# Gated product and attention sum kept in PSUM, chunk-0 scores by heads at partitions 0 and 64, and a new order list, in an mLSTM-then-gated-FFN kernel

## Chip, cores and metric

One core of a Trainium2 chip. The metric is device time in microseconds; the kernel before takes 550.04 us (median of 3 runs).

## The reference

Two stages. The first is an mLSTM over 768 steps for 4 batches and 8 heads of width 40, the second a gated feed-forward layer on its output (3072 tokens, 320 features, 1536 hidden).

```
for t in range(S):
    m_new = maximum(f[t] + m, i[t]);  fs = exp(f[t] + m - m_new);  is_ = exp(i[t] - m_new);  m = m_new
    C = fs * C + is_ * v_t k_t^T;     n = fs * n + is_ * k_t
    y[t] = sigmoid(o[t]) * (C q_t) / max(|n . q_t|, 1)
x    = y rearranged to (B*S, H*D)
out  = (sigmoid(x @ w_gate) * (x @ w_val)) @ w_out
```

## The kernel before

Time is cut into 6 chunks of 128 steps (c). A *unit* n = 4c + b is one chunk of one batch b: 24 units, each with all 8 heads. Within a chunk the recurrence is turned into attention: scores of k against q, times a decay matrix `d`, times v (with a column of ones for the denominator), plus, from chunk 1 on, the part that comes from the carried state `cst`. The output of a unit, 128 tokens, is split into two fp32r parts `xh` and `xl`, which the feed-forward layer multiplies with weights that are split in the same way.

Each operation is a small function with a name, and the list `ORDER` names all of them in the order in which they are recorded. Each engine runs its own instructions in that order, waiting for what they read and for the buffers that they write. The names that matter here (n a unit or a tile, g a group of heads, x a half):

- `lq`, `lk`, `lv`, `lo`, `ld`: loads of q, k, v, the output gate and the decay's row maxima, on SP's queue (the first q on ACT's). `wd..`, `wa..`, `wb..`, `wc..`, `wo..`, `wh..`, `wl..`: load and split of a piece of the weights (letter g, v, r, o: gate, value, the last 64 features of both, output).
- `tr n.g`: TensorE transposes of q and k of a group of heads to PSUM (`pt`); `cp n.g`: copy to SBUF (`qkt`); `qb n.g`: the q of the group, repeated per head and multiplied by a mask, so that it becomes block-diagonal (`qbd`); `s n.g`: the scores, one fp32 matmul per group of 3, 3 and 2 heads (`GROUPS`). Chunks 0 and 1 work like this. From chunk 2 on (`tq`, `tw`, `sr`, `sh`, `sl`) q and k are transposed by way of DRAM, and `sl` (L662) finishes an exact split on DVE.
- `sp`, `ee`, `em`: decay of units 0 and 1; `t n.g`: scores times decay, on DVE (L777); `dl`, `kw`: k times the last decay column, for the state; `cs`, `cm`, `cd`, `ca`: state update; `in`, `ti`: state part of the output, in tile `t`; `av n`: decay-weighted scores times v (L837, L844).
- `ad n` (L852): `t` + `av`; `nd n`: the denominator, three small DVE steps; `ns n`: times the output gate; `ro n`: divided; `xd`, `xt`, `xh`, `xl`: transpose and split of the result.
- feed-forward tile n (128 hidden features j, and 2 or 4 units, so 256 or 512 tokens): `u0`, `r0`: 8 matmuls for the gate into bank `pg0`; `u1`, `r1`: 8 for the value into `pg1`; `th`: tanh of the gate to tile `sg` (L977, ACT); `gx`: (sg + 1) * value (L981, DVE); `gh`: its high part (L986, ACT); `gl`: the rest (L991, DVE); `dn n.t`: three matmuls per unit into the output bank `po t`. `ob`: output to DRAM.

PSUM has eight banks: `po0` to `po3`, `pg0`, `pg1`, and `pa0`, `pa1`, which take turns for everything else. Some early operations borrow the first six (`POPEN`). `sg` has one buffer, `gh` and `gl` two. `wm` is 8 matmuls on zeros, whose result nobody reads. In chunk 0 the masks of unit 0 (three) and one each of units 1, 2 and 3 run on DVE, the other six on POOL.

Of the kernel before, what the change touches and what calls it, by code (L numbers as in the profile page):

```python
# [8 lines left out]
F32 = mybir.dt.float32  # L9
# [18 lines left out]
    'BC': 2,  # L28
    'warm': 8,
# [14 lines left out]
    qb1.2 wdo3 cp2.0 lq4 dl1 wbg0 xd0 s1.1 l11 wdv1 wcg0 wog0 whv0 wlo1 whg0 tr2.1 og1 t1.0 ld3 cp2.1 s1.2 t1.2 t1.1
    wlv0 xt0 xh0 xl0 wdv2 ee2.1 qb2.1 av1 wao3 wbo3 ns1 qb2.0 s2.0 nd1 em2 ro1 wlg0 xd1 dl2 xt1 wav1 wco3 wao2 ee3.0
    t2.0 xh1 kw1 wbv1 tr2.2 cp2.2 lq6 woo3 who3 l12 kw2 wlo3 wag1 xl1 u1.0 ee3.1 lo4 cs1 cm1.0 wbo2 wco2 wcv1 cm1.1
    woo2 wov1 lv4 l14 whv1 wbg1 u0.0 em3 tr3.0 r0.0 wcg1 ld4 who2 cp3.0 tr3.1 wlo2 qb2.2 wog1 wdo4 r1.0 cp3.1 th0
    tr3.2 s2.2 gx0 cp3.2 lo2 t2.2 gh0 s2.1 t2.1 lk4 dl3 tbp tbc wlv1 og2 qb3.1 wao4 ee4.0 whg1 wbo4 wlg1 u0.1 av2
    tr4.1 lv3 l13 wco4 lo3 gl0 qb3.2 og4 og3 woo4 r0.1 u1.1 ns2 th1 who4 qb3.0 nd2 tr4.0 cp4.0 cp4.1 r1.1 wdr1 wlo4
    ld6 war1 s3.1 t3.1 wav2 s3.0 wbr1 t3.0 ee4.1 wdv3 qb4.0 tr4.2 gx1 qb4.1 u0.2 s3.2 t3.2 ro2 cp4.2 av3 ee6.1 gd  # L50
    cs2 wcr1 u1.2 xd2 ns3 nd3 lk5 wbv2 tdp wcv2 dn0.0 gh1 cm2.0 cm2.1 wor1 wov2 tdc em4 dl4 wdo5 s4.1 qb4.2 t4.1
    wdr2 lv5 s4.0 t4.0 dn0.1 s4.2 whr1 wdg4 xt2 t4.2 wao5 xh2 xl2 wbo5 wlr1 r1.2 lq5 wco5 woo5 r0.2 kw4 cs4 whv2
    war2 av4 l15 cm4.0 wdr3 cm4.1 gl1 in4 kw3 wbr2 wcr2 who5 ro3 xd3 i6 wlv2 th2 u0.3 wdg3 wor2 wlo5 dn1.0 dn1.1 ti4
    wdo7 gx2 u1.3 r0.3 gh2 ad4 xt3 gl2 ld5 r1.3 tr5.0 dn2.0 th3 xh3 dn2.1 gx3 xl3 u0.4 wav3 wag4 cp5.0 r0.4 tr5.1
    gh3 whr2 wbv3 wcv3 wov3 wdg2 cs3 gl3 wbg4 u1.4 r1.4 cp5.1 whv3 dn3.0 th4 gx4 u0.5 r0.5 dn3.1 gh4 gl4 th5 tep
    u1.5 r1.5 dn4.2 wcg4 wlr2 wao7 wog4 gx5 u0.6 wbo7 dn4.3 r0.6 wlv3 wag2 u1.6 wbg2 wcg2 r1.6 ee5.0 gh5 wog2 whg2
    gl5 dn5.3 dn5.2 th6 u0.7 r0.7 wco7 gs4 gx6 u1.7 wlg2 r1.7 gh6 gl6 ns4 th7 gs5 woo7 nd4 whg4 gx7 lq8 wlg4 u0.8
    cm3.0 cm3.1 gh7 gl7 wdv5 dn6.2 who7 u1.8 r0.8 qb5.0 wag3 wbg3 wlo7 qb5.1 dn6.3 dn7.3 th8 r1.8 war3 wbr3 u0.9
    dn7.2 r0.9 gx8 wcr3 wcg3 wog3 wdv4 ro4 wor3 wdo6 gh8 gl8 s5.1 u1.9 r1.9 whg3 wlg3 whr3 wlr3 th9 dn8.1 wav4 lk6
    gs2 tec gx9 wbv4 dn8.2 gh9 lo5 cd4.0 dn8.3 wdo8 u0.10 wcv4 cd4.1 ca4.1 dn8.0 ee6.0 ee5.1 tr5.2 r0.10 wov4 u1.10  # L60
    r1.10 whv4 gl9 wao6 dn9.3 wbo6 lo6 th10 lv6 wao8 em5 wco6 dl5 gx10 woo6 u0.11 dn9.0 r0.11 wdr4 u1.11 dn9.1 r1.11
    kw5 dn9.2 who6 wlv4 wbo8 wco8 wdg5 woo8 gh10 gl10 who8 wlo8 war4 wlo6 th11 wav5 t5.1 xd4 gx11 wbr4 wcr4 s5.0
    cp5.2 u0.12 wbv5 dn10.0 wor4 t5.0 wdo9 qb5.2 whr4 wlr4 dn10.2 lk7 dn10.3 gh11 em6 in5 tr6.0 ti5 cp6.0 wcv5 wov5
# [127 lines left out]
def mlstm_then_gated_ffn_kernel(  # L191
# [87 lines left out]
    taken["gh"] = 1  # L279

    @op("wz")
    def _():
        nc.vector.memset(warm, 0.0)
# [248 lines left out]
    def unit(n):  # L532
# [313 lines left out]
        def hs():  # L846
            return t1s[n] if c > 0 else pv_[n]
# [207 lines left out]
```

## Time and profile before

| | |
|---|---|
| runs | 550.04 us median of 3 (548.8 to 552.62) |
| profiled execution, as timed / its span | 546.66 us / 544.9 us |
| TensorE (PE) | 518.4 us busy, 95% |
| VectorE (DVE) | 360.5 us, 66% |
| ScalarE (ACT) | 248.0 us, 46% |
| GpSimdE (POOL) | 266.2 us, 49% |
| moved by DMA | 74.15 MB, mean 136 GB/s |
| granted clock, mean | 0.984 |

Busy is the time in which an engine has an instruction in work. A row of the order of time reads: start, duration, engine, line, operation, output <- inputs, shape, count, and in brackets how long the engine stood idle just before and what ended that. A row of a group has, behind the bar, busy time, mean of one in ns, idle time before them and its releasers. A row of waits has the time in all, the times and the longest.

### The profile page before, as it was taken

The page shows a single profiled execution, that of the slowest core. Times are in us where ns is not written, and L with a number is a line of the kernel's source. Part 1 is how long each engine was busy: PE and PEld are TensorE (multiplying, and loading weights), DVE is VectorE, ACT ScalarE, POOL GpSimd, SP SyncE. Part 2 cuts the span into 40 slices and gives each one's busy share as a digit, 9 for nine tenths or more (in the row PEclk, how much of TensorE's full clock was granted, in tenths as well). Part 3 has the DMA queues.
Part 4 walks back from the last instruction along what each step waited for, and adds up shares of the span by engine and source line. Part 5 has one row for each costly group of instructions (what it writes and reads, how often), then busy time and mean ns, then how long its engine had stood idle before and what let it go on. Part 6 is the DMA issues. An engine that isn't in the chain of part 4 may idle for free.

```text
span 544.9 us, 10878 instructions
## 1 busy us (share of the span) xinstructions
PE 518.4 (95%) x3957; PEld 472.7 (87%) x3957; DVE 360.5 (66%) x702; ACT 248.0 (46%) x564; POOL 266.2 (49%) x299
## 2 busy tenths in 40 slices
PE   5889999999989999989989999999999979999997
PEld 4668998889989999988778888888888878899997
DVE  7888877777877667657767467677555675744232
ACT  4867666654525453553432444441444322423222
POOL 2767555748464564574763756835502436421000
PEclk9959999999999999999998999999999999999999
DMA  9985836467587878696684779775786485221000
GB/s 209 254 226 138 235 86 147 125 143 171 159 156 147 166 169 173 119 201 148 145 173 92 161 164 188 143 128 128 133 162 118 85 153 103 52 38 50 6 14 36
DMA packets 222477, 74.15 MB, mean 136 GB/s; under 512 B 167380, under 2 KB 214168, under 8 KB 222424
## 3 DMA queue, kind: packets, MB, share of 16 engines
q1 hardware_dynamic: 221336, 73.20, 62.4%
q8 instruction: 31, 0.51, 0.4%
q10 hardware_dynamic: 1088, 0.26, 0.3%
q14 instruction: 22, 0.18, 0.1%
HBM read 61.54 MB, written 11.90 MB: 135 GB/s over the span
## 4 chain that ended last, share of the span: by engine, by line
PE 69%; DMA 13%; SPq 6%; DVE 5%; issue 3%; ACT 3%; POOL 1%; ACTq 0%; DVEq 0%; POOLq 0%
PE pg L967 28%; PE po L1001 6%; PE po L1003 6%; PE po L1002 6%; PE pg L971 5%; PE pg L972 5%; DMA scx<-tx 3%; DMA qs<-scq 3%; PE av L837 2%; PE s L679 2%; DMA d<-mscr 2%; PE s L713 2%; PE av L844 2%; PE in L820 2%; SPq L650 1%
## 5 line engine op out<-in xcount | busy, mean ns | idle before, releaser
L967 PE MATMUL pg<-xh,wh 128*128 128x256 f32 (+1 forms) x412 | 106.8, 341 | 6.7 <-ACT sg L977 5.6
L981 DVE SCALAR_TENSOR_TENSOR sg<-sg,pg 128x256 f32<-128x256 f32 (+1 forms) x103 | 53.8, 523 | 74.7 <-PE pg L972 50.0
L986 ACT ACTIVATE gh<-sg 128x256 fp32r<-128x256 f32 (+1 forms) x103 | 51.7, 502 | 112.3 <-DVE sg L981 83.8
L967 PE MATMUL pg<-xh,wl 128*128 128x256 f32 (+1 forms) x412 | 101.8, 329 | 0.0
L967 PE MATMUL pg<-xl,wh 128*128 128x256 f32 (+1 forms) x412 | 101.7, 328 | 0.0
L977 ACT ACTIVATE sg<-pg 128x256 f32<-128x256 f32 (+1 forms) x103 | 48.1, 467 | 109.5 <-PE pg L972 54.5
L991 DVE TENSOR_TENSOR gl<-sg,gh 128x256 fp32r<-128x256 f32 (+1 forms) x103 | 71.1, 690 | 40.1 <-ACT gh L986 39.8
L1001 PE MATMUL po<-oh,gh 128*128 128x320 f32 x288 | 92.3, 321 | 0.0
L1003 PE MATMUL po<-oh,gl 128*128 128x320 f32 x288 | 89.5, 311 | 0.5 <-DVE gl L991 0.5
L1002 PE MATMUL po<-ol,gh 128*128 128x320 f32 x288 | 89.1, 309 | 0.0
L967 PEld LDWEIGHTS pg<-xh,wh 128*128 128x128 f32 x412 | 67.9, 191 | 12.8 <-ACT sg L977 7.7
L967 PEld LDWEIGHTS pg<-xl,wh 128*128 128x128 f32 x412 | 69.8, 191 | 7.5 <-POOL xl L910 0.6
L967 PEld LDWEIGHTS pg<-xh,wl 128*128 128x128 f32 x412 | 69.9, 191 | 7.1
L971 PE MATMUL pg<-xh,w 128*128 128x256 f32 (+1 forms) x206 | 69.2, 338 | 0.0
L972 PE MATMUL pg<-xl,w 128*128 128x256 f32 (+1 forms) x206 | 67.0, 327 | 0.0
L1001 PEld LDWEIGHTS po<-oh,gh 128*128 128x128 f32 x288 | 54.5, 189 | 2.7
L1002 PEld LDWEIGHTS po<-ol,gh 128*128 128x128 f32 x288 | 54.3, 189 | 2.8
L1003 PEld LDWEIGHTS po<-oh,gl 128*128 128x128 f32 x288 | 54.2, 188 | 1.0 <-DVE gl L991 1.0
L793 POOL TENSOR_TENSOR dr<-d 128x1024 f32<-128x1024 f32 x16 | 31.8, 1986 | 44.5 <-DVE d L777 44.5
L777 DVE TENSOR_TENSOR d<-s,d 128x384 f32<-128x384 f32 (+1 forms) x72 | 35.5, 504 | 12.6 <-PE s L679 7.0
L612 POOL TENSOR_TENSOR d<-at,d 128x1024 f32<-128x1024 f32 x16 | 33.0, 2068 | 21.8 <-DMA d<-mscr 17.4
L620 POOL TENSOR_SCALAR_AFFINE_SELECT d<-d 128x1024 f32<-128x1024 f32 x22 | 25.9, 1180 | 36.0 <-ACT d L616 31.9
(151 smaller groups left out, 936.1 us busy)
## 6 DMA issues: line engine op xcount, KB each, us to landing
d<-mscr SPq DMA_DIRECT2D x22, 512.0 KB
ks<-scq SPq DMA_DIRECT2D x48, 168.0 KB
qs<-scq SPq DMA_DIRECT2D x48, 168.0 KB
scq<-tq SPq DMA_DIRECT2D x64, 80.0 KB
k<-in_k_dram SPq DMA_DIRECT2D x24, 160.0 KB
su_o<-in_moe_w_out_dram SPq DMA_DIRECT2D x12, 320.0 KB
v<-in_v_dram SPq DMA_DIRECT2D x24, 160.0 KB
o<-in_o_gate_dram SPq DMA_DIRECT2D x24, 160.0 KB
```

Source lines behind the costliest of these rows:

```text
L612: E("ea", n).tensor_tensor(dm[n], a, dm[n], ALU.subtract)
L777: nc.vector.tensor_tensor(y, ps_[n, g][:, :nh, :], y, ALU.mult)
L967: nc.tensor.matmul(p, w[y][:, a, fs], x[c][:, a, n0:n1], start=(i + a == 0), stop=False)
L971: nc.tensor.matmul(pg[n, y], w2[y][:, fs], xh[c][:, 2, n0:n1], start=False, stop=False)
L972: nc.tensor.matmul(pg[n, y], w2[y][:, fs], xl[c][:, 2, n0:n1], start=False, stop=True)
L977: nc.scalar.activation(s, pg[n, 0], AF.Tanh, scale=0.5)
L981: nc.vector.scalar_tensor_tensor(sgs[n], sgs[n], 1.0, pg[n, 1], ALU.add, ALU.mult)
L986: nc.scalar.activation(ghs[n][:, :nt], sgs[n], AF.Copy)
L991: E("gl", n).tensor_tensor(gls[n][:, :nt], sgs[n], ghs[n][:, :nt].bitcast(F32), ALU.subtract)
L1001: nc.tensor.matmul(p, ghs[n][:, ts], oh[:, j, :], start=(j == 0), stop=False)
L1002: nc.tensor.matmul(p, ghs[n][:, ts], ol[:, j, :], start=False, stop=False)
L1003: nc.tensor.matmul(p, gls[n][:, ts], oh[:, j, :], start=False, stop=(j == NF - 1))
```

## The change

Four parts.

1. `gx` writes its product over the value in `pg1`; `gh` and `gl` read it from there. `sg` is then read only by `gx`.
2. `ad` writes its sum over `av` in PSUM; `nd` and `ns` read it there.
3. In chunk 0, q and k are loaded with each head's 40 columns padded to 64 (the pads are zeroed by DVE, `pz`; the tiles borrow buffers of `xh`, `xl`, `gl`, `gh` and `sg`). A transpose takes two heads, which come to lie at partitions 0 and 64; there are four for q and four for k of a unit, into two banks. A score matmul takes one head from partitions 0 to 39 or 64 to 103 and writes to one of two banks. `qb`, the third group of `tr`, `cp`, `s` and `t`, and the block-diagonal q go for these units. `kw` writes to a new tile.
4. A new `ORDER`, and other borrowed banks. The parameters `CA` and the per-half lookup for `cd` are there and change nothing.

```diff
+    'GX': 1, 'AD': 1, 'CA': 0, 'PAD': 1,
...
+        pads = []
+        for x, tags in enumerate((("xh1",), ("xl1",), ("gl0", "gl1"), ("gh1", "sg0"))):
+            ts = [sb.tile([P, 2 // len(tags), H, DP], F32, tag=t, name=f"pad{x}{y}") for y, t in enumerate(tags)]
+            pads.append([ts[y][:, 0] if len(tags) == 2 else ts[0][:, y] for y in range(2)])
+        @op("pz")
+            for w in pads[0] + pads[1] + pads[2] + pads[3]:
+                nc.vector.memset(w[:, :, D:], 0.0)
...
     POPEN = {
         "sp0.0": "po0", "sp0.1": "po1", "sp1.0": "po2", "sp1.1": "po3",
-        "tr0.2": "pg0", "tr1.0": "pg0", "tr1.1": "pg1", "s0.0": "pg1", "s1.0": "po1", "s1.1": "po2", "s1.2": "po3",
-        "av0": "po0", "av1": "pg0",
+        "s0.0": "pg0", "s0.1": "pg1", "s1.0": "po0", "s1.1": "po1", "av0": "pg0", "av1": "pg1",
...
+            for x in range(2):                                      # tr, cp of a padded unit
+                    pt_[n, x] = p = pst(P_(f"tr{n}.{x}"), [P, 4, L], f"pt_{n}_{x}")
+                    for y in range(4):
+                        nc.tensor.transpose(p[:, y, :], pads[n][x][:, 2 * y : 2 * y + 2, :].rearrange("p h d -> p (h d)"), ident)
...
+            @op(f"s{n}.0")
+                for x in range(2):
+                    ps_[n, x] = pst(P_(f"s{n}.{x}"), [P, 4, L], f"s_{n}_{x}")
+                for y in range(4):
+                    for x in range(2):
+                        rs = slice(DP * x, DP * x + D)
+                        nc.tensor.matmul(ps_[n, x][:, y, :], sop[n][rs, 1, y, :], sop[n][rs, 0, y, :], start=True, stop=True)
...
-                y = dm[n][:, h0 : h0 + nh, :]
+                y = dm[n][:, g::2, :] if padded else dm[n][:, h0 : h0 + nh, :]
                 nc.vector.tensor_tensor(y, ps_[n, g][:, :nh, :], y, ALU.mult)
...
+                if padded:
+                    kt[n] = sbt("k", [P, H, D], F32, f"k_{n}", 3)
...
-            return t1s[n] if c > 0 else pv_[n]
+            return t1s[n] if c > 0 and not PARAM["AD"] else pv_[n]
...
-                nc.vector.tensor_tensor(t1s[n], t1s[n], pv_[n], ALU.add)
+                nc.vector.tensor_tensor(hs(), t1s[n], pv_[n], ALU.add)
...
-            nc.vector.scalar_tensor_tensor(sgs[n], sgs[n], 1.0, pg[n, 1], ALU.add, ALU.mult)
+            gate = sgs[n]
+            if PARAM["GX"]:
+                sgs[n] = pg[n, 1]
+            nc.vector.scalar_tensor_tensor(sgs[n], gate, 1.0, pg[n, 1], ALU.add, ALU.mult)
```

What the new list does is shown at three places. The **first** is TensorE ahead of the first feed-forward matmul. Here `pt` are the transposes, `s` the scores, `xt` the transposes of a unit's result, `pg_0` the first tile. Before:

```order
L713 MATMUL s_2_376<-qbd_212,qkt_211 128x256
L899 MATMUL xt_381<-ident,x_340 128x128 x3
L844 MATMUL av_396<-v_290,d_186 128x41 x8
L713 MATMUL s_0_410<-qbd_350,qkt_349 128x384
L899 MATMUL xt_423<-ident,x_417 128x128 x3
L690 MATMUL pt_2_440<-ident,q_245 80x128
L690 MATMUL pt_2_440<-ident,k_218 80x128
L967 MATMUL pg_0_454<-xh_385,wh_96 128x256 x2
```

Now (behind the last row come seven more score matmuls of unit 2, alternating between banks, and then the first tile, value first as before):

```order
L706 MATMUL pt_1_312<-ident,pad_96 128x128 x4
L706 MATMUL pt_0_323<-ident,pad_95 128x128 x4
L893 MATMUL av_347<-v_197,d_186 128x41 x8
L893 MATMUL av_357<-v_317,d_200 128x41 x8
L706 MATMUL pt_0_371<-ident,pad_97 128x128 x4
L948 MATMUL xt_393<-ident,x_388 128x128 x3
L379 MATMUL pwarm<-warm 128x128 x8
L948 MATMUL xt_428<-ident,x_424 128x128 x3
L725 MATMUL s_0_442<-qkt_343 128x128
```

The two `av` follow one another, and the matmuls on zeros (`pwarm`) moved from ahead of unit 0's last scores to between the two results' transposes. The **second** place is TensorE in the last chunk, behind the value matmuls of tile 95 (`r1`). Names in `wh_93`/`wh_99` are gate weights, `wh_96`/`wh_102` value weights, `po` output banks. Before:

```order
L967 MATMUL pg_96_6888<-xh_6132,wh_93 128x256 x2
L967 MATMUL pg_96_6888<-xh_6132,wl_94 128x256 x2
L967 MATMUL pg_96_6888<-xl_6133,wh_93 128x256 x2
L971 MATMUL pg_96_6888<-xh_6132,w_95 128x256
L972 MATMUL pg_96_6888<-xl_6133,w_95 128x256
L967 MATMUL pg_96_6898<-xh_6132,wh_96 128x256 x2
```

Now:

```order
L1062 MATMUL po_5_6726<-oh,gh_6858 128x320
L1063 MATMUL po_5_6726<-ol,gh_6858 128x320
L1064 MATMUL po_5_6726<-oh,gl_6878 128x320
L1062 MATMUL po_5_6732<-oh,gh_6858 128x320
L1063 MATMUL po_5_6732<-ol,gh_6858 128x320
L1064 MATMUL po_5_6732<-oh,gl_6878 128x320
L1025 MATMUL pg_96_6897<-xh_6211,wh_99 128x256 x2
L1025 MATMUL pg_96_6897<-xh_6211,wl_100 128x256 x2
L1025 MATMUL pg_96_6897<-xl_6212,wh_99 128x256 x2
L1029 MATMUL pg_96_6897<-xh_6211,w_101 128x256
L1030 MATMUL pg_96_6897<-xl_6212,w_101 128x256
L1025 MATMUL pg_96_6911<-xh_6211,wh_102 128x256 x2
```

Two output groups of the tile before stand between the value of tile 95 and the value of tile 96; before there was only the gate of tile 96. The **third** place is DVE around unit 0's decay product (`d<-s,d`), with the weight steps of `dc_v` (the first value weights) beside it. Before:

```order
L487 TENSOR_SCALAR dc_v_161<-dc_v_161 128x512
L706 TENSOR_TENSOR qbd_133<-qkt_132,bmask 120x384
L706 TENSOR_TENSOR qbd_212<-qkt_211,bmask 120x384
L492 SCALAR_TENSOR_TENSOR dc_o_153<-su_o_117,dc_o_153 128x320
L492 SCALAR_TENSOR_TENSOR dc_v_161<-st_v_147,dc_v_161 128x512
L783 COPY dl_242<-d_173 128x8
L777 TENSOR_TENSOR d_173<-s_1_234,d_173 128x384
```

Now:

```order
L501 TENSOR_SCALAR dc_v_164<-dc_v_164 128x512
L716 COPY qkt_147<-pt_1_215 128x512
L506 SCALAR_TENSOR_TENSOR dc_v_164<-st_v_154,dc_v_164 128x512
L402 SCALAR_TENSOR_TENSOR mg<-gin,mend 32x128
L403 TENSOR_TENSOR mend<-gin,mg 32x1
L829 COPY dl_273<-d_186 128x8
L823 TENSOR_TENSOR d_186<-s_1_258,d_186 128x4x128
```

The two masks are gone, the copy of the transposes takes 512 columns in one step, and a decay product takes four heads.

More of the change, by code (lines that the diff above doesn't have):

```diff
@@ L28 @@
     'BC': 2,
+    'GX': 1,
+    'AD': 1,
+    'CA': 0,
+    'PAD': 1,
     'warm': 8,
@@ L44 @@
[L44 to L63, printed above, removed]
@@ new lines @@
+    dn93.3 ob5.1 u0.95 r0.95 dn93.2 gl94 u1.95 r1.95 dn94.3 dn94.2 th95 u0.96 r0.96 gx95 gh95 gl95 u1.96 r1.96 th96
+    dn95.3 dn95.2 u0.97 r0.97 gx96 gh96 gl96 u1.97 r1.97 dn96.2 th97 gx97 gh97 dn96.3 u0.98 r0.98 gl97 u1.98 r1.98
+    dn97.2 th98 dn97.3 u0.99 r0.99 gx98 gh98 gl98 u1.99 r1.99 th99 u0.100 r0.100 gx99 dn98.2 gh99 dn98.3 gl99 th100
+    u1.100 r1.100 gx100 gh100 gl100 u0.101 dn99.2 r0.101 th101 dn99.3 u1.101 r1.101 gx101 u0.102 gh101 dn100.2 gl101
+    r0.102 u1.102 r1.102 th102 gx102 dn100.3 dn101.3 dn101.2 gh102 gl102 dn102.3 dn102.2 ob5.3 ob5.2
@@ L278, in mlstm_then_gated_ffn_kernel @@
     warm = sb.tile([P, 2 * P], F32, tag="gh0", name="warm")
-    taken["gh"] = 1
+    taken["gh"] = 0 if PARAM["PAD"] else 1
     @op("wz")
@@ L283, in _ @@
         nc.vector.memset(warm, 0.0)
+    if PARAM["PAD"]:
+        DP = 64
+        pads = []
[3 more added lines that the diff above has]
+        @op("pz")
+        def _():
+            for w in pads[0] + pads[1] + pads[2] + pads[3]:
+                nc.vector.memset(w[:, :, D:], 0.0)
     @op("lf")
@@ L540, in unit @@
         spread = n < PARAM["BC"]
+        padded = c == 0 and PARAM["PAD"]
         def rows(t):
@@ L549, in _ @@
         def _():
-            qt[n] = sbt("q", [P, H, D], F32, f"q_{n}", 3)
+            qt[n] = pads[n][0][:, :, :D] if padded else sbt("q", [P, H, D], F32, f"q_{n}", 3)
             (nc.scalar if n == 0 else nc.sync).dma_start(qt[n], rows(q))
@@ L554, in _ @@
         def _():
-            kt[n] = sbt("k", [P, H, D], F32, f"k_{n}", 3)
+            kt[n] = pads[n][1][:, :, :D] if padded else sbt("k", [P, H, D], F32, f"k_{n}", 3)
             nc.sync.dma_start(kt[n], rows(k))
@@ L679, in _ @@
                         nc.tensor.matmul(p[:, m, :], stk[n, 1][: 3 * DX, h0 + m, :], stk[n, 0][: 3 * DX, h0 + m, :], start=True, stop=True)
+        elif padded:
+            hl = "hl"[b % 2]
+            for x in range(2):
+                @op(f"tr{n}.{x}")
+                def _(x=x):
+                    pt_[n, x] = p = pst(P_(f"tr{n}.{x}"), [P, 4, L], f"pt_{n}_{x}")
+                    for y in range(4):
+                        nc.tensor.transpose(p[:, y, :], pads[n][x][:, 2 * y : 2 * y + 2, :].rearrange("p h d -> p (h d)"),
+                                            ident)
+                @op(f"cp{n}.{x}")
+                def _(x=x):
+                    if n not in sop:
+                        sop[n] = sbt(f"b{hl}", [P, 2, 4, L], F32, f"qkt_{n}")
+                    if is_act(f"cp{x}", n):
+                        nc.scalar.activation(sop[n][:, x], pt_[n, x], AF.Copy)
+                    else:
+                        nc.vector.tensor_copy(sop[n][:, x], pt_[n, x])
+            @op(f"s{n}.0")
+            def _():
+                for x in range(2):
[4 more added lines that the diff above has]
+                        nc.tensor.matmul(ps_[n, x][:, y, :], sop[n][rs, 1, y, :], sop[n][rs, 0, y, :], start=True, stop=True)
         elif not stacked:
@@ L771, in _ @@
                                               sc[:, 0, :, x, :].rearrange("m d w -> d m w"))
-        for g, (h0, nh) in enumerate(GROUPS):
+        for g, (h0, nh) in enumerate(((0, 4), (1, 4)) if padded else GROUPS):
             @op(f"t{n}.{g}")
             def _(g=g, h0=h0, nh=nh):
-                y = dm[n][:, h0 : h0 + nh, :]
+                y = dm[n][:, g::2, :] if padded else dm[n][:, h0 : h0 + nh, :]
                 nc.vector.tensor_tensor(y, ps_[n, g][:, :nh, :], y, ALU.mult)
@@ L929, in _ @@
                 @op(f"cd{n}.{y}")
-                def _(cv=cv, gs=gs, r=r, ng=ng, w=w):
-                    E("cd", n).tensor_tensor(cv, cv, cdec[:r, c, b, gs].unsqueeze(2).broadcast_to([r, ng, w]), ALU.mult)
+                def _(cv=cv, gs=gs, r=r, ng=ng, w=w, y=y):
+                    E(f"cd{y}", n).tensor_tensor(cv, cv, cdec[:r, c, b, gs].unsqueeze(2).broadcast_to([r, ng, w]), ALU.mult)
+            if c > 0 and PARAM["CA"]:
+                @op(f"ca{n}.{y}")
+                def _(cv=cv, gs=gs, r=r, w=w):
+                    for j in range(w // DA):
+                        js = slice(j * DA, (j + 1) * DA)
+                        nc.vector.scalar_tensor_tensor(cv[:, :, js], pc_[n][:r, gs, js], rmask[:r, j : j + 1], cv[:, :, js],
+                                                       ALU.mult, ALU.add)
+                continue
             @op(f"cm{n}.{y}")
```

260 lines of the change are left out of this document (138 added, 122 removed).

## Prediction

> **What bounds the kernel now.** I read the page's first part, then busy time by stretches, then who waited for whom, then the order of time where TensorE stood still. In the second block a row is a stretch: its length, each engine's busy time, the granted clock, the DMA share and GB/s.
>
> ```profile
> PE 518.4 (95%) x3957; PEld 472.7 (87%) x3957; DVE 360.5 (66%) x702; ACT 248.0 (46%) x564; POOL 266.2 (49%) x299
> ```
> ```profile
> core 0: us, PE busy (x) PEld busy (x) DVE busy (x) ACT busy (x) POOL busy (x), PEclk, DMA share, GB/s
> 14.00:26.00 12.00, 10.29 (x68) 7.76 (x66) 9.48 (x25) 9.48 (x30) 8.73 (x14) 1.00 1.06 258
> 26.00:40.00 14.00, 11.70 (x48) 9.40 (x47) 11.75 (x23) 9.39 (x30) 9.59 (x14) 0.51 0.83 225
> 150.00:300.00 150.00, 142.83 (x1303) 134.35 (x1303) 106.32 (x205) 64.06 (x140) 83.75 (x90) 0.99 0.76 154
> 400.00:530.00 130.00, 125.78 (x992) 117.65 (x992) 67.84 (x125) 45.37 (x89) 34.81 (x31) 1.00 0.37 74
> 530.00:545.00 15.00, 11.47 (x90) 11.21 (x88) 3.88 (x9) 3.97 (x10) 0.00 (x0) 1.00 0.09 33
> ```
>
> TensorE is the bound: 518.4 of the span's 544.9 us (95%). A change can win only what it does not work (26.5 us), what it works slowly, or work itself. The second block says where that is. From 26 to 40 us the granted clock is 0.51, so 11.70 us of matmuls there would be about 6 at full clock: some 5 us lost, in the start. Between 150 and 300 us 7.2 us are idle, between 400 and 530 us 4.2, and 3.5 in the tail, which waits for the last output. The other half of the idle time lies before 42 us.
>
> ```profile
> PE pg L967 <- ACT sg L977: 5.6, 5, 2.1
> PE s L679 <- issue: 2.8, 1, 2.8
> ACT sg L977 <- DVE gl L991: 51.8, 44, 3.9
> ```
> ```profile
> 282.63 0.67 DVE L991 TENSOR_TENSOR gl<-sg,gh 128x512 fp32r<-128x512 f32 x1
> 283.39 0.60 ACT L977 ACTIVATE sg<-pg 128x512 f32<-128x512 f32 x1 [2.41 <-DVE gl L991]
> 284.04 0.73 PE L967 MATMUL pg<-xh,wh 128*128 128x512 f32 x2 [2.15 <-ACT sg L977]
> ```
>
> These rows show one cause of the later idle time. The tile sg has one buffer. It is free only when gl has read it, the next tanh (L977) waits for that, and the next gate matmul waits for the tanh, because pg0 is one bank. ACT waited so 44 times; five times it reached TensorE, for 5.6 us.
>
> **The change, part by part.**
>
> *Product in PSUM.* gx now writes into its own bank pg1, and gh and gl read it there. sg is free one step after the tanh, so the wait above goes: 5.6 us. What it adds is a wait of the next value matmul (pg1 is one bank too) for gl instead of gx. The durations of that chain:
>
> ```profile
> L991 DVE TENSOR_TENSOR gl<-sg,gh 128x512 fp32r<-128x512 f32 x41 | 36.9, 901 | 17.6 <-ACT gh L986 17.6
> L991 DVE TENSOR_TENSOR gl<-sg,gh 128x256 fp32r<-128x256 f32 x62 | 34.2, 551 | 22.5 <-ACT gh L986 22.2
> L981 DVE SCALAR_TENSOR_TENSOR sg<-sg,pg 128x512 f32<-128x512 f32 x41 | 28.0, 683 | 29.4 <-PE pg L972 21.9 <-ACT sg L977 6.9 <-ACT d L616 0.4
> L986 ACT ACTIVATE gh<-sg 128x512 fp32r<-128x512 f32 x41 | 25.9, 631 | 62.2 <-DVE sg L981 44.3 <-PE po L1002 16.3 <-PE po L1003 1.5
> ```
> ```profile
> 508.91 0.31 PE L1003 MATMUL po<-oh,gl 128*128 128x320 f32 x1
> 509.06 0.28 PE L971 MATMUL pg<-xh,w 128*128 128x256 f32 x1
> 509.18 0.28 PE L972 MATMUL pg<-xl,w 128*128 128x256 f32 x1
> 509.56 0.42 DVE L981 SCALAR_TENSOR_TENSOR sg<-sg,pg 128x256 f32<-128x256 f32 x1 [1.46 <-PE pg L972]
> 510.47 0.42 DVE L991 TENSOR_TENSOR gl<-sg,gh 128x256 fp32r<-128x256 f32 x1 [0.49 <-ACT gh L986]
> ```
>
> Where nothing disturbs it, the chain of a 256-wide tile is 1.43 us (509.46, the end of its last matmul, to 510.89). In the new list two 320-wide output groups stand between (the second place shown above): 8 matmuls of a gate tile at 0.12 us (509.06 to 509.18) and 6 output matmuls at 0.15 (508.91 to 509.06) are 1.86 us of cover, 0.4 more than needed. In the old list cover fell to 0.96, which the shorter wait allowed and the longer one would not. A 512-wide tile needs 0.68 + 0.63 + 0.67 + 0.15 for handovers, 2.1 us; the least cover that I count in the new list, at twice the 0.12 for a 512-wide matmul, is about 2.6 (a gate tile and an `in`). So gl must not be held up by more than about 0.4 us. It will be, sometimes: DVE runs in order, and its queue holds steps like these:
>
> ```profile
> L662 DVE SCALAR_TENSOR_TENSOR ks<-ks,rsign,kt 126x1024 fp32r<-126x1024 f32 x16 | 23.9, 1491 | 6.9 <-ACT kt L656 5.6 <-DMA scq<-tq 1.2
> L662 DVE SCALAR_TENSOR_TENSOR qs<-qs,rsign,qt 126x1024 fp32r<-126x1024 f32 x16 | 21.5, 1346 | 10.0 <-ACT qt L656 10.0
> ```
>
> I give 1.6 us back for this, two such steps less the margin. gl itself should be shorter. Its 901 and 551 ns are those of two SBUF operands beside a busy POOL; 0.67 and 0.42 are shown above where it was undisturbed, and gx, with one operand in PSUM, is near its undisturbed time throughout (683). Some 17 us of DVE work go (41 x 0.22 + 62 x 0.13), behind TensorE, so they count nothing by themselves.
>
> *Attention sum in PSUM.* ad, nd and ns work on the bank of av, for 20 units. nd and ns of chunk 0 read PSUM already, so their prices are known:
>
> ```profile
> L858 DVE SCALAR_TENSOR_TENSOR den<-av,den 128x8 f32<-128x8 f32 x4 | 0.7, 166 | 0.1
> L863 DVE SCALAR_TENSOR_TENSOR o<-o,av 128x320 f32<-128x320 f32 x4 | 1.9, 486 | 1.2 <-PE av L844 1.1
> ```
>
> They hold a pa bank (there are two) for three small steps and one of 0.49 us longer, about 1.0 us per unit. Whoever takes that bank next stands at least 2.4 us of TensorE work behind av in the new list, counted as above. I cost it at nothing; uncovered it would be up to 1 us in a unit.
>
> *Chunk 0.* The mask multiplies qb of four units go (6 on DVE, 6 on POOL), the 24 transposes become 32, the 12 score matmuls become 32 with 40 rows each. The score columns stay 1024 per unit. Two transposes more per unit at 0.11 us (0.22 for two) cost 0.4 us for units 2 and 3, which lie where TensorE is the bound; for units 0 and 1 they count in the start. Eight memsets of the pads (192 columns each) are new on DVE: at most 3.4 us by the 0.42 of a 256-wide step, while q and k are still landing. Uncovered they would delay the start by that much, which its lower end takes in. The masks were a link of the start's chain, below. The row of the transposes, from the chain that ended last:
>
> ```profile
> 13.35 0.22 PE pt L690 x2
> ```
>
> *The start* is the largest term. Rows of before:
>
> ```profile
> 9.06 0.66 ACT L478 ACTIVATE dc_v<-st_v 128x512 f32<-128x512 f32 x1 [0.95 <-DMA st_v<-in_moe_w_val_dram]
> 9.89 1.14 ACT L587 ACTIVATE d<-mb,at 128x128 f32<-128x128 f32 x4
> 14.84 0.37 ACT L699 ACTIVATE qkt<-pt 120x256 f32<-120x256 f32 x1
> 16.36 0.86 ACT L504 ACTIVATE w<-dc_r 64x256 fp32r<-64x256 f32 x2
> 17.37 1.99 PE L713 MATMUL s<-qbd,qkt 120*128 120x384 f32 x6
> 19.01 0.47 ACT L812 ACTIVATE o<-o 128x320 f32<-128x320 f32 x1 [1.39 <-DMA o<-in_o_gate_dram]
> 19.20 1.88 PE L844 MATMUL av<-v,d 128*128 128x41 f32 x16
> 20.90 0.81 PE L920 MATMUL cs<-v,k 128*120 128x123 f32 x6
> 21.28 0.73 POOL L706 TENSOR_TENSOR qbd<-qkt,bmask 80x256 f32<-80x256 f32 x1
> 25.64 3.44 PE L844 MATMUL av<-v,d 128*128 128x41 f32 x16 [0.39 <-issue]
> 34.50 0.80 PE L967 MATMUL pg<-xh,wh 128*128 128x256 f32 x2 [0.99 <-ACT xh L906]
> 39.81 0.28 PE L972 MATMUL pg<-xl,w 128*128 128x256 f32 x1
> ```
>
> The rows are of the order of time. The first gate matmul (34.50) waits for unit 1: its last mask multiply at 21.28, its av at 25.64, which took 3.44 us at half clock against 1.7 for unit 0 (19.20 to 20.90), and then 5.4 us (29.08 to 34.50) for normalisation, transpose and split. In the new order the same chain, by the same prices:
> - Transfers. 1,604 KB are issued up to the weights that land at 9.06, 3,942 KB up to the o that lands at 19.01: 235 KB per us. The o of unit 1 now has 4,868 KB up to it (4,262 before), so it lands at 19.01 + 926/235 = 22.9 us, ahead of its use.
> - ACT from 9.7 us: four groups of exponentials (4 x 1.14), weight steps (0.86 for a pair, and half of that once more), a wait for the DVE step ahead of the first of them (0.7, estimated) and two copies of 512 columns (0.6 each, estimated from 0.37 for 256) end at about 17.5. Then the scores of unit 1 can run.
> - TensorE from 17.5: scores 1.83 (17.37 to 19.20 is the same number of columns), cs 0.65, eight transposes 0.88, av twice 1.7: 24.3 at full clock, 31.0 at half. It idles about 2.4 us ahead of that and is then busy without a break. In before the clock came back about 5 us after 34.50; I take half clock for the first 4.5 us: 26.5.
> - The tail of 5.4 us, unchanged: first gate matmul at about **32**, against 34.5, a lead of 2.5. Of before, the two transposes and two score groups that followed the first tile up to 42 us (1.9 us from its end, 39.81 + 0.28) are done by then in the new order.
>
> That makes 4.4; I take **4.5**, with ends 0 and 7 (31.0 and 24.3 in place of 26.5). What is pushed back for it (weights, o and k of units 2 and 3) costs nothing while it lands in time; the lower end holds the case that it doesn't.
>
> The Trainium skill, "TensorE: Matmul & The Clock Gate", Part 1, says that the clock halves after about 3.4 us of an idle window and is full again after about 3.4 us busy. The trace agrees on the half (0.51) and shows about 5 us for the return. By that rule the 2.4 us gap would not throttle at all and the lead would be some 6.6 us, an estimate.
>
> **Sum**, against the profiled execution's 546.66 us: start -4.5, gate waits -5.6, new waits for gl +1.6, transposes +0.4: -8.1, that is 538.6. The median of the runs is 550.04, 3.4 above the profiled execution; minus 8.1 it is **541.9 us**.
>
> **Rivals.**
> 1. *The start gives nothing.* TensorE stays at half clock to the end of the chain (31.0 for the two av instead of 26.5), or the gate weights, 512 KB behind the o of unit 1, set the time. For it: DMA share 1.06 and 0.83 before 40 us. Then -3.6: 546.4. Chance 0.22.
> 2. *Slower: the value bank becomes the wait.* If half of the 32 long DVE steps (L662) fall between a gx and its gl, each takes 1.4 - 0.5 us from TensorE: +14, and 556 in all. It decides once gl is late by more than 0.4 us in most tiles. Against it: the cover is 1.8 us or more nearly everywhere. Chance 0.10.
> 3. *More than forecast.* The largest idle piece after 42 us (2.8, ahead of scores) goes too, the start gains 7, nothing is given back for gl, and the score matmuls at partitions 0 and 64 run two at a time, half of 1.83 us for each of units 2 and 3. Together -7 -5.6 -2.8 -1.8 +0.4 = -16.8: 533. Chance 0.18.
>
> The Trainium skill, "TensorEngine Tiling (Array Packing)", says both that two 64-row tiles run independently (Overview) and that switching the tiling mode drains the engine (Key Properties). No row here shows either; by the first the sum would be 1.8 us less, by the second up to that much is given back.
>
> **How the numbers follow.** Forecast with its spread (start 2 to 6, waits +-3): 537 to 546, chance 0.50. The range **531 to 551** takes in rival 1 and most of rival 3. A difference under 1% (544.5 to 555.5) is about what cannot be told from none here. Faster by more: nine tenths of the forecast and all of rival 3, 0.63. Slower by more: most of rival 2 with a tail, 0.09. Between: 0.28.
>
> **What would show it.** First gate matmul near 32 us; the stretch at clock 0.5 shorter; no wait of the tanh for gl; waits of the value matmul for gl of a microsecond or two in all; gl near 0.67 and 0.42; qb on 12 instructions. Wrong would be: the first gate matmul at 34 or later, a large sum of waits for gl at pg1, or new waits for transfers that eat the lead.

## The result, and the profile after

The changed kernel takes **533.63 us** (median of 4 runs, 532.81 to 536.6) against 550.58 us before (4 runs, 548.8 to 552.62): ratio 0.970, 95% interval 0.965 to 0.975. In a second comparison, with five rounds, it was 534.98 us against 548.52 us, ratio 0.974 (0.970 to 0.977). The forecast was 541.9 us in a range of 531 to 551. The profiled execution took 532.81 us with a span of 531.1, so 13.8 us less span than before.

The first part of the page, after:

```profile
PE 514.0 (97%) x4005; PEld 474.4 (89%) x4005; DVE 333.9 (63%) x700; ACT 244.1 (46%) x560; POOL 251.9 (47%) x293
```

Busy time by stretches, cut where the start ends (the last stretch runs to the end of the span). Before:

```profile
0.00:42.00 42.00, 31.32 (x159) 25.05 (x159) 32.59 (x77) 26.37 (x78) 24.10 (x44) 0.84 0.95 226
42.00:600.00 558.00, 487.10 (x3800) 447.65 (x3800) 327.87 (x626) 221.63 (x487) 242.13 (x256) 1.00 0.55 116
```

After:

```profile
0.00:42.00 42.00, 33.72 (x225) 30.91 (x225) 32.26 (x79) 26.25 (x75) 21.21 (x41) 0.84 0.86 214
42.00:600.00 558.00, 480.29 (x3782) 443.45 (x3781) 301.62 (x622) 217.86 (x487) 230.66 (x253) 1.00 0.55 117
```

This is the ledger of the gain. At 42 us TensorE has 6.8 us less work ahead of it (480.29 against 487.10), and of the rest of the span it idles 8.8 us (531.1 - 42 - 480.3) where it idled 15.8 (544.9 - 42 - 487.1): 7.0 us less. Together 13.8. Both clocks up to 42 us read 0.84, so between these two executions the start did not win by its clock.

What TensorE waits for after (waits, longest in total first; then two waits of other engines):

```profile
PE tat L423 <- DVE gin L385: 4.7, 1, 4.7
PE av L886 <- DVE t L874: 1.4, 1, 1.4
PE s L725 <- ACT qkt L714: 1.4, 1, 1.4
PE s L697 <- issue: 0.9, 1, 0.9
...
PE po L1064 <- DVE gl L1052: 0.2, 1, 0.2
```
```profile
ACT sg L1035 <- PE pg L1030: 61.0, 63, 3.8
DVE gl L1052 <- ACT gh L1047: 31.7, 59, 1.2
```

The 5.6 us behind the tanh are gone; the tanh waits for matmuls now, not for gl. And the new wait that was feared, the value matmul (L1025) for gl, has no row for TensorE; only three weight loads of L1025 wait for gl, 0.8 us in all. Why gl is hardly ever late stands in its durations (min, median, max in ns), before and after:

```profile
L991 DVE TENSOR_TENSOR gl<-sg,gh x103: 381/656/2427, 43.8 to 540.0; 128x256 fp32r<-128x256 f32 x62, 128x512 fp32r<-128x512 f32 x41
```
```profile
L1052 DVE TENSOR_TENSOR gl<-pg,gh x103: 384/425/693, 42.3 to 526.3; 128x256 fp32r<-128x256 f32 x62, 128x512 fp32r<-128x512 f32 x41
```

The fastest step is the same; the longest fell from 2.43 to 0.69 us. Of the 103 steps of before 15 took over 1 us, after none.

The start after, on TensorE:

```profile
14.29 1.16 PE L725 MATMUL s<-qkt 40*128 40x128 f32 x16
16.81 1.29 PE L725 MATMUL s<-qkt 40*128 40x128 f32 x16 [1.36 <-ACT qkt L714]
21.60 6.89 PE L893 MATMUL av<-v,d 128*128 128x41 f32 x32
29.90 2.72 PE L379 MATMUL pwarm<-warm 128*128 128x128 f32 x16
32.46 0.49 PE L948 MATMUL xt<-ident,x 128*128 128x128 f32 x3
35.21 0.50 PE L1025 MATMUL pg<-xh,wh 128*128 128x256 f32 x2
```

The first gate matmul starts at 35.21 us, later than the 34.50 of before; but unit 2 has been transposed and scored by then, and the clock is full already. A unit's eight score matmuls take 1.16 us at full clock, where as many columns took 1.99 before (the row at 17.37 us). The trace records each of these matmuls twice, hence x16.

### The profile page after: what moved, and what is told of

It reads as the page before. It is cut to its first block, busy times and chain, and to the rows that moved or that the text cites. A ratio compares the mean times of both kernels' runs of the same rounds, so it can differ in the third digit from the quotient of the medians.

```text
span 531.1 us, 10974 instructions
## 1 busy us (share of the span) xinstructions
PE 514.0 (97%) x4005; PEld 474.4 (89%) x4005; DVE 333.9 (63%) x700; ACT 244.1 (46%) x560; POOL 251.9 (47%) x293
## 4 chain that ended last, share of the span: by engine, by line
PE 79%; DMA 7%; SPq 4%; ACT 3%; DVE 3%; issue 2%; POOL 2%; DVEq 0%; POOLq 0%; ACTq 0%
PE pg L1025 33%; PE po L1062 7%; PE po L1064 6%; PE po L1063 6%; PE pg L1029 5%; PE pg L1030 5%; PE av L893 3%; PE av L886 3%; PE s L697 2%; PE cs L969 2%; PE in L869 2%; DMA scx<-tx 2%; DMA qs<-scq 2%; SPq L647 2%; PE s L759 1%
## 5 line engine op out<-in xcount | busy, mean ns | idle before, releaser
L1042 DVE SCALAR_TENSOR_TENSOR pg<-sg,pg 128x256 f32<-128x256 f32 (+1 forms) x103 | 54.8, 532 | 98.1 <-PE pg L1030 72.4
L1047 ACT ACTIVATE gh<-pg 128x256 fp32r<-128x256 f32 (+1 forms) x103 | 48.2, 468 | 139.7 <-DVE pg L1042 122.5
L1025 PE MATMUL pg<-xh,wh 128*128 128x256 f32 (+1 forms) x412 | 105.8, 338 | 0.3 <-ACT xh L955 0.2
L1025 PE MATMUL pg<-xh,wl 128*128 128x256 f32 (+1 forms) x412 | 101.2, 327 | 0.0
L1025 PE MATMUL pg<-xl,wh 128*128 128x256 f32 (+1 forms) x412 | 100.9, 326 | 0.0
L1062 PE MATMUL po<-oh,gh 128*128 128x320 f32 x288 | 94.3, 327 | 0.3 <-ACT gh L1047 0.3
L1025 PEld LDWEIGHTS pg<-xl,wh 128*128 128x128 f32 x412 | 69.1, 190 | 7.5 <-POOL xl L959 0.6
L1025 PEld LDWEIGHTS pg<-xh,wl 128*128 128x128 f32 x412 | 69.0, 189 | 7.2
L1052 DVE TENSOR_TENSOR gl<-pg,gh 128x256 fp32r<-128x256 f32 (+1 forms) x103 | 54.1, 526 | 33.0 <-ACT gh L1047 31.7
L1025 PEld LDWEIGHTS pg<-xh,wh 128*128 128x128 f32 x412 | 67.1, 189 | 3.8 <-DVE gl L1052 0.8
L842 POOL TENSOR_TENSOR dr<-d 128x1024 f32<-128x1024 f32 x16 | 30.3, 1894 | 52.8 <-DVE d L823 50.6
L823 DVE TENSOR_TENSOR d<-s,d 128x384 f32<-128x384 f32 (+2 forms) x68 | 34.9, 526 | 12.7 <-PE s L697 7.3
L630 POOL TENSOR_TENSOR d<-at,d 128x1024 f32<-128x1024 f32 x16 | 31.3, 1959 | 22.5 <-DMA d<-mscr 18.8
```

The source lines that it names most:

```text
L630: E("ea", n).tensor_tensor(dm[n], a, dm[n], ALU.subtract)
L823: nc.vector.tensor_tensor(y, ps_[n, g][:, :nh, :], y, ALU.mult)
L1025: nc.tensor.matmul(p, w[y][:, a, fs], x[c][:, a, n0:n1], start=(i + a == 0), stop=False)
L1042: nc.vector.scalar_tensor_tensor(sgs[n], gate, 1.0, pg[n, 1], ALU.add, ALU.mult)
L1047: nc.scalar.activation(ghs[n][:, :nt], sgs[n], AF.Copy)
L1052: E("gl", n).tensor_tensor(gls[n][:, :nt], sgs[n], ghs[n][:, :nt].bitcast(F32), ALU.subtract)
```

## The experiments

All times are medians beside the kernel before in the same comparison (548.5 to 550.3 us); differences from the new kernel go by ratios, with 0.974 for it. Where an edit breaks the order that a buffer's reuse needs, the operations concerned were moved by as little as that needs; their number is given.

**The halves of the list.**

```diff
 start_alone:  ORDER = new list to chunk 0's last score step + old list;  GX 0, AD 0, PAD 1
 rest_alone:   ORDER = old list to chunk 0's last score step + new list;  GX 1, AD 1, PAD 0
```

> The new list up to the end of chunk 0's scores, with the pads, and the old list behind it; the product and the attention sum in SBUF as before (8 operations of the old list had to move behind the last reader of a buffer). Theory 1, the gain is about half in the start: in the two profiles the TensorE work left at 42 us is 487.1 us before and 480.3 after, so this kernel is 5 to 8 us faster than before, about 543 us against 550, and keeps the later waits of the tanh for gl (5 to 6 us). Rival: the lead of the start is lost again to later waits for transfers and the gain is all in the rest of the list: then within 2 us of before.

> The old list with masks and three score groups up to the end of chunk 0's scores, and the new list behind it, with the product and the attention sum in PSUM. Theory 1: idle time of TensorE after 42 us goes from 15.8 to about 9 us, so 6 to 8 us faster than before, about 543 us, with the start of before (first gate matmul near 34.5 us). Rival: all of the gain is here: 13 us or more, 537 us. The two halves together should give the 13.8 us between the two profiles if nothing ties them.

Measured: 558.39 us, ratio 1.016 (1.007 to 1.026), and 565.66 us, ratio 1.033 (1.025 to 1.041). Each half alone is slower than before, which neither theory had. At the joint TensorE idles 4.6 us between 42 and 100 us in the one and 10.6 in the other, and the clock halves again there (49.19 to 62.84 us in `start_alone`). The split fails as a split: the parts do not add. (In `rest_alone` 43 operations moved, in `start_alone` 8.)

**The product in PSUM, in either list.**

```diff
 old_list_product_psum:  old kernel and list with 'GX': 1   (95 operations moved)
 new_list_product_sbuf:  new kernel and list with 'GX': 0   (22 operations moved)
```

> The product in PSUM alone, in the old list; where the old list has the next value matmuls ahead of gl, the bank would never come free, so these matmuls stand behind gl there (95 operations of 2,724 moved). Theory 1, the change of place only trades one wait for another, and the new list is what pays: the waits of the tanh for gl go (5.6 us), value matmuls wait for gl for 4 us or more in all, time within 4 us of before. Rival: the change of place alone is the gain of the middle: waits for gl under 2 us and 4 to 6 us faster.

> The new kernel with the product in SBUF again (sg with one buffer); 22 operations moved so that a tanh stands behind the gl that frees sg. Theory 1, the list needs the freed sg: the tanh waits for gl again and TensorE loses 4 to 7 us to it, about 539 us. Rival: the list alone does it and the place of the product does not matter: within 2 us of the new kernel, and TensorE waits for the tanh under 2 us.

Measured: 584.18 us, ratio 1.066 (1.058 to 1.074), and 554.81 us, ratio 1.008 (1.003 to 1.013). The waits of TensorE, first in the old list with the product in PSUM (this profiled execution lies 10 us above the median), then in the new list with the product in SBUF, with its gl steps, the longest of them, one of the POOL steps beside it, and the matmul that waited for it:

```profile
PE pg L1027 <- DVE gl L1054: 28.8, 37, 2.0
```
```profile
PE po L1064 <- DVE gl L1052: 6.0, 6, 3.4
PE pg L1025 <- ACT sg L1035: 5.5, 5, 2.3
```
```profile
L1052 DVE TENSOR_TENSOR gl<-sg,gh x103: 381/678/4267, 43.9 to 548.7; 128x256 fp32r<-128x256 f32 x62, 128x512 fp32r<-128x512 f32 x41
```
```profile
196.71 4.27 DVE L1052 TENSOR_TENSOR gl<-sg,gh 128x256 fp32r<-128x256 f32 x1
198.81 1.89 POOL L842 TENSOR_TENSOR dr<-d 128x1024 f32<-128x1024 f32 x1
201.03 0.41 PE L1064 MATMUL po<-oh,gl 128*128 128x320 f32 x1 [3.43 <-DVE gl L1052]
```

In the old list the bank pg1 is the wait, 28.8 us of it: the change of place, with the 95 moves that it needs there, costs 34 us. In the new list it is worth 19 us (554.8 against 535). Theory 1 named the right waits and was far off in size: it had within 4 us for the old list, and 4 to 7 us for the new. In the new list the output matmuls wait for gl too, since gl in SBUF takes up to 4.27 us: that step starts at 196.71 us, POOL works without a break from 196.41 to 200.69, and gl ends at 200.98. Behind each of TensorE's three longest waits after 42 us (2.26, 3.43 and 1.64 us) stands a stretch at half clock (123.17 to 126.58, 201.68 to 205.09 and 358.69 to 362.1 us).

**The sum in PSUM, in either list.**

```diff
 new_list_sum_sbuf:  new kernel and list with 'AD': 0   (none moved)
 old_list_sum_psum:  old kernel and list with 'AD': 1   (66 operations moved)
```

> The new kernel with the attention sum in SBUF again; the list is the same. Theory 1, its place is worth nothing by itself: within 1.5 us of the new kernel, no new wait of TensorE over 0.5 us. Rival: the shorter steps on PSUM are part of the slack of DVE: 3 us or more slower.

> The attention sum in PSUM alone, in the old list; 66 of 2,724 operations moved, because nd and ns now have to stand ahead of the next user of the bank. Theory 1: the bank held longer makes whoever takes it next wait, 1 us in some of the 20 units: 3 to 12 us slower than before. Rival, as in the prediction: it costs nothing, within 2 us.

Measured: 548.71 us, ratio 0.999 (0.995 to 1.002), 14 us slower than the new kernel, and 569.17 us, ratio 1.034 (1.029 to 1.040). The rival held in the new list, and Theory 1 failed there. The step of nd that reads t in SBUF (min, median, max), the same step on the bank of av in the new kernel, and the longest one on DVE with POOL's work in that time and the matmul that came late by it:

```profile
L906 DVE TENSOR_SCALAR den<-t x20: 154/166/3184, 75.9 to 490.1; 128x8 f32<-128x8 f32 x20
```
```profile
L906 DVE TENSOR_SCALAR den<-av x24: 148/158/167, 25.6 to 474.3; 128x8 f32<-128x8 f32 x24
```
```profile
340.60 3.18 DVE L906 TENSOR_SCALAR den<-t 128x8 f32<-128x8 f32 x1
...
340.22 1.89 POOL L846 TENSOR_TENSOR ds<-dr 128x1024 bf16<-128x1024 f32 x1
342.07 0.59 POOL L980 TENSOR_TENSOR cst<-cst,cdec 120x246 f32<-120x246 f32 x1
342.61 0.11 POOL L583 MEMSET v<- 128x8 f32 x1
342.67 1.09 POOL L638 TENSOR_SCALAR_AFFINE_SELECT d<-d 128x1024 f32<-128x1024 f32 x1
...
346.61 0.19 PE L886 MATMUL av<-v,d 128*128 128x41 bf16 x1 [2.90 <-DVE t L874]
```

A step on eight columns, 0.16 us of work, ends at 343.78 us, when POOL's last step of four in a row ends (343.76). In PSUM none of the 24 took over 0.17. DVE's steps behind it come late, an attention product waits 2.90 us for one of them, and from 348.02 to 351.43 us the clock is half. That is one place; after 42 us TensorE idles 18.0 us in this run (547.2 - 42 - 487.2) against 8.8, in many small waits. In the old list, where 66 operations had to move, the edit costs 20 us, more than the 3 to 12 of Theory 1; this run cannot tell the moves from the bank held longer.

The 19 us of the product and the 14 us of the sum make 33, about twice the whole gain. They are not shares of it: each is what this list loses when one part is taken out, and with either part out nothing is left of the gain. The new list with both tiles in SBUF was not run, so what the list would give by itself is open.

**Scores that lie side by side.**

```diff
-                for y in range(4):
-                    for x in range(2):
+                for x in range(2):
+                    for y in range(4):
                         rs = slice(DP * x, DP * x + D)
```

> The new kernel with the score matmuls of a unit in another order: the four head pairs of partitions 0 to 39 first and then the four of 64 to 103, instead of alternating. Theory 1, neighbours at partitions 0 and 64 overlap (16 records took 1.16 us, against 1.88 for the 16 mask-product score columns of before): a unit's scores take about 1.8 us instead of 1.2, 0.6 us per unit, 1 to 2.5 us slower in all. Rival: they do not overlap, the shorter time is from 40 rows instead of 120: scores stay at 1.2 us, time within 0.5 us.

Measured: 538.3 us, ratio 0.981 (0.977 to 0.985), about 4 us slower than the new kernel. (The 1.88 in the expectation is the row of an attention product; the scores' row of before is 1.99.) TensorE:

```profile
14.09 1.71 PE L725 MATMUL s<-qkt 40*128 40x128 f32 x16
...
37.54 0.50 PE L1025 MATMUL pg<-xh,wh 128*128 128x256 f32 x2
```

The same eight matmuls (16 records) take 1.71 us instead of 1.16 when neighbours use the same partitions, so alternating ones overlap: 0.55 us per unit at full clock. The edit changes the order of the two banks too; that was not tested apart. The first gate matmul comes 2.3 us later, and the half clock lasts one stretch longer (17.29 to 34.36 us), but most of that is not shown to be the edit's. `new_list_sum_sbuf` has the list and the start of the new kernel, and there too the clock was half for 17.07 us (16.93 to 34.00) and the first gate matmul came late:

```profile
36.97 0.50 PE L1025 MATMUL pg<-xh,wh 128*128 128x256 f32 x2
```

In `new_list_product_sbuf` it was 17.07 us as well, with the gate matmul at 36.84. One and the same start thus differs by 1.8 us from one execution to another, and 0.6 us are left for the order of the scores.

**The fillers and the half clock.**

```diff
 no_warm:           'warm': 8 -> 0
 warm_gap:          + "wn" (six products on zeros, bank po0) ahead of s1.0
 warm_gap_v_early:  as warm_gap, lv1 four loads earlier
 fill_two_gaps:     as warm_gap_v_early, "wm" with 3 products, in bank po2
 new_again:         the new kernel
```

> The new kernel without its eight filler products (pwarm, which compute nothing that is used). In the new kernel they take TensorE from 29.9 to 32.4 us, between the two token transposes, and the half clock ends at 31.4. Theory A, they only cost: the second token transpose could start at 31.1 and all behind it comes 1.2 us earlier, about 532.4 us. Theory B, the granted clock comes back after a stretch of 3.41 us that TensorE fills with wide matmuls, and these products are that stretch: without them the half clock lasts 3.4 us or more longer (17.1 us instead of 13.65) and the kernel is 0 to 3 us slower.

> The new kernel with six more filler products ahead of unit 1's scores, in the idle 1.36 us of TensorE before 16.81 us. Theory B, the half clock that begins at 17.9 us follows a stretch of 3.41 us in which TensorE idled about 1.9 us; with the gap filled it begins 3.4 us later or more and the two attention products (6.7 us at half clock) run partly at full clock: 2 to 4 us faster, about 530.5 us. Rival: the clock halves for another reason (the attention products of 41 columns count as little work): half clock from the same time or soon after, within 1 us of the new kernel.

> The new kernel unchanged, as the control of the others: every theory says 533 to 535 us and the half clock of 13.65 us from 17.9 us on.

> The new kernel with six more filler products ahead of unit 1's scores, as in the run warm_gap (there: half clock of 6.83 us instead of 13.65, first gate matmul at 34.23 us), and the load of unit 1's v issued four loads earlier, since its attention product waited 1.11 us for it there. Theory B: half clock 6.83 us again, no wait for v, first gate matmul near 33.2 us, and 1 to 2.5 us faster than the new kernel in the same comparison. Rival: what the start gains is lost later, since the rest of the list is fitted to the old lead: within 1 us of the new kernel or slower, with 3 us or more of new idle time after 42 us.

> As warm_gap_v_early (fillers ahead of unit 1's scores, v of unit 1 early), and of the eight old fillers only three are left, in a bank that is free, so that they run in the gap of 1 us after the first token transpose (25.9 us) and do not stand in the way of the second, which could start near 27.1 us. Theory B, a stretch filled with 128-column matmuls brings the clock back: half clock of 3.4 to 6.8 us, first gate matmul at 30 to 31.5 us instead of 33.58. If the lead lasts, 2 to 4 us faster than the new kernel, about 531.5 us; rival: it is lost again after 42 us as that of warm_gap_v_early was, 534 to 537 us.

| run | us | ratio | half clock in the start, us | first gate matmul |
|---|---|---|---|---|
| new_again | 534.98 | 0.974 (0.970 to 0.977) | (no profile of use: that execution took 821.52 us) | |
| no_warm | 538.09 | 0.981 (0.977 to 0.985) | 17.80 to 41.69 | 35.32 |
| warm_gap | 537.23 | 0.979 (0.975 to 0.984) | 23.95 to 30.78 | 34.23 |
| warm_gap_v_early | 536.53 | 0.977 (0.973 to 0.981) | 24.40 to 31.23 | 33.58 |
| fill_two_gaps | 537.53 | 0.975 (0.968 to 0.982) | 22.33 to 29.16 | 31.68 |

The stretches of 3.41 us in the start of the new kernel (TensorE's busy time is the second number), and two of `no_warm`:

```profile
14.30:17.71 3.41, 2.05 (x33) 1.86 (x32) 2.74 (x6) 3.34 (x9) 3.17 (x5) 1.00 1.02 260
17.71:21.12 3.41, 3.05 (x18) 2.43 (x15) 3.34 (x7) 2.19 (x9) 3.26 (x7) 0.50 1.17 201
21.12:24.54 3.42, 3.42 (x19) 3.42 (x17) 2.03 (x6) 3.22 (x11) 1.61 (x3) 0.50 1.00 294
24.54:27.96 3.42, 3.42 (x18) 3.42 (x17) 2.15 (x8) 0.80 (x2) 0.31 (x1) 0.50 0.46 148
27.96:31.37 3.41, 3.41 (x17) 3.16 (x17) 2.25 (x8) 1.91 (x4) 0.20 (x1) 0.50 0.48 176
```
```profile
28.04:31.45 3.41, 2.16 (x10) 1.78 (x11) 2.38 (x9) 2.00 (x4) 0.31 (x1) 0.50 0.46 171
...
38.28:41.69 3.41, 3.41 (x18) 3.41 (x18) 2.50 (x6) 1.48 (x6) 0.79 (x2) 0.50 0.57 147
```

Theory B holds for `no_warm`: without the fillers the stretch from 28 us is not filled (2.16 of 3.41) and the half clock lasts 23.9 us instead of 13.65 (or 17.07, as in the two runs above), until a stretch full of gate matmuls. By the ratios it is 4 us slower, where Theory B had 0 to 3. It holds for `warm_gap` as far as the clock: with the gap filled the half clock begins 6.2 us later and lasts half as long. But none of the three filled versions is faster than the control, where 1 to 4 us had been expected if the lead lasts. `fill_two_gaps` leads by 3.5 us at the first gate matmul, and has 478.24 us of TensorE work left at 42 us, 2.0 less than the new kernel; after 42 us it idles 11.6 us (531.8 - 42 - 478.2) against 8.8:

```profile
PE pg L1031 <- DVE gl L1058: 1.6, 1, 1.6
PE av L892 <- DVE t L880: 1.4, 1, 1.4
PE pt L742 <- ACT ct L1004: 1.0, 1, 1.0
```

All five other versions of this start that were profiled idle 11.4 to 12.7 us after 42 us. The times are those of the rival, by which a lead in the start is lost again. How much of this is the list's and how much the day's is open, since the control has no usable profile.

## Why the prediction came out as it did

The time lies in the range, and near the **third rival** (-16.8) rather than the forecast (-8.1). That its total came so close is in part luck: it had the gate waits and nothing for gl right, but its start of 7 was 5.1, its idle piece of 2.8 us ahead of scores is 0.9 now, and it had neither the attention sum nor the half clock behind a stall. By steps:

- **The start, -4.5.** The size was about right, the path was not. The step that failed is "I take half clock for the first 4.5 us". The half clock lasted 13.65 us in both profiles, so the two attention products took 6.9 us at half clock, to 28.49 instead of 26.5, and the first gate matmul came at 35.21 instead of 32, which the prediction itself names as a sign of being wrong (34 or later). About 2.0 of these 3.2 us are the half clock and 1.3 the tail, 6.7 us where I took 5.4: unit 1's result is transposed behind the fillers, at 32.46, 4.0 us after its attention product (2.8 before). Scores of unit 1 at 16.81 (17.5 forecast) were near. What the start did win stands in the ledger: of the 6.8 us less work at 42 us, 1.7 are a later stretch at half clock (next point) and 5.1 are the start's: 2.4 of less idle time (33.72 busy against 31.32), about 2 of cheaper scores (0.7 for each of three units), and 0.6 that I cannot assign. Whether all of it reaches the end is not shown; `fill_two_gaps` says that a further lead did not. And it holds for this pair of executions: the same start was 1.8 us later in `new_list_sum_sbuf`.
- **Gate waits, -5.6, and new waits for gl, +1.6.** The first was right; the second should have been about 0. (Its 1.6 is also not the sum of its own numbers: two steps of 1.4 us, each less the margin of 0.4, are 2.0.) I took gl's time from its mean and its undisturbed rows, and the margin of 0.4 us from DVE's queue. The rows on record had the sign of the real danger, a gl slowed beside POOL, but it was the spread, up to 2.43 us, that the place in PSUM took away. Mis-sized besides: a stall of 2 us can cost more than itself. Behind the stall of 2.15 us at 284 the clock of before was half for 3.41 us, which is 1.7 us of work lost:

```profile
282.04:285.45 3.41, 1.41 (x6) 1.19 (x7) 3.27 (x10) 2.05 (x3) 1.13 (x2) 1.00 0.88 195
285.45:288.86 3.41, 3.41 (x13) 2.80 (x12) 3.06 (x4) 1.48 (x6) 1.55 (x2) 0.50 0.11 41
```

  With these 1.7 and the 7.0 of idle time the middle gave 8.7 where the two terms gave 4.0.
- **The attention sum at nothing.** Wrong: the new list is 14 us slower without it (`new_list_sum_sbuf`). The bank held longer is what I priced; that DVE's steps no longer stretch beside POOL is what counted, as far as the one step followed above shows.
- **Scores.** Their cost was taken as unchanged, with the overlap only in the third rival (1.8 us for units 2 and 3). It is about 0.7 us less per unit (1.16 against 1.83 from the first start to the next matmul's), 0.55 of it by the overlap.
- **Rival 2** is real, and it is what the same edit does to the old list: 28.8 us of waits at pg1. In 56 of the 102 steps from one tile to the next the old list has the next value matmul ahead of gl itself, so there gl has no cover at all; the new list has it so in none, and its cover was enough.
- **Rival 1** was right that the chain would run at half clock to its end, and wrong that the start gives nothing: 5.1 us by the ledger.

By the Trainium skill, "TensorE: Matmul & The Clock Gate", Part 1, activity is watched in free-running windows of 3,413 ns, which agrees with half clocks of 3.41, 6.83, 13.65, 17.07 and 23.89 us here. Its rule that an idle window halves the clock would have left the gap of this start alone; here 2.05 us busy of 3.41 were too little, so the measurement decides. The Trainium skill, "SBUF — State Buffer", Who interferes with whom, says that GpSimd and DVE steps that take the shared ports lock each other out for a whole instruction. The 3.18 us step that ends with POOL's agrees, except that it lasted through several POOL steps in a row and not one.

## What to carry to other kernels

Look at the longest time of a step that others wait for, not at its mean: an operand moved to PSUM changed DVE's fastest step by nothing and its longest from 2.43 to 0.69 us, and in the new list that decided. Before a buffer is held longer, count the work that the order puts between its release and its next use: the same edit cost 34 us in a list that had left none in 56 places and had to be changed for it, and was worth 19 in one that leaves some everywhere. Price a stall of about 2 us on TensorE with the half clock that can follow it, 1.7 us more. And do not read a difference of 2 us in the start from one profile each: with no change to it the half clock lasted 13.65 us in one execution and 17.07 in two others.

## What the runs showed of the hardware

- The half clock comes in whole stretches of 3.41 us. It followed stretches in which TensorE was busy 1.41 and 2.05 us (rows above), but not one of before with 1.92 us, after its idle 2.75 us at 444.6, so busy time alone does not set it:

```profile
445.87:449.29 3.42, 1.92 (x12) 1.74 (x13) 2.76 (x6) 0.63 (x1) 1.89 (x1) 1.00 0.77 209
```

- Being busy is not enough to end it: two stretches filled with attention products of 41 columns (3.42 us busy each, rows above) stayed at half clock; the one filled with transposes and fillers of 128 columns ended it, and without the fillers one of gate matmuls did. That narrow products count as little work fits, but was not tested by itself. In `warm_gap_v_early` a stretch fully busy with them at full clock was followed by the half clock too:

```profile
20.99:24.40 3.41, 3.41 (x33) 3.41 (x33) 3.24 (x12) 3.27 (x10) 2.05 (x4) 1.00 1.05 247
24.40:27.81 3.41, 2.40 (x11) 1.72 (x10) 2.91 (x11) 2.07 (x6) 0.15 (x1) 0.50 1.00 358
```
- Matmuls of 40 rows at partitions 0 and 64 overlap when they alternate: eight in 1.16 us against 1.71.
- A DVE step of eight columns on SBUF lasted 3.18 us beside four POOL steps in a row, and one of 256 columns with two SBUF operands 4.27 us; the first never took over 0.17 us on PSUM, the second never over 0.69 with one operand there.
